# Second-layer matmuls of a fused attention and feed-forward kernel: three passes behind every product, or six behind every second one

## The chip, the cores and the metric

The kernel runs on one core of a Trainium2 chip. The metric is the device time of one execution in microseconds (us). Engines are named as in the profile: PE (TensorE, matmuls), PEld (its weight loads), DVE (VectorE), ACT (ScalarE), SP (SyncE, which issues the DMAs here). A *pass* below is one matmul instruction on PE with 512 moving columns (480 in the last pair of a batch).

## The reference

Four batches of channel attention are followed by a feed-forward layer with GELU:

```python
qn = q / (norm(q, axis=1) + 1e-06); kn = k / (norm(k, axis=1) + 1e-06)   # q, k, v: 4 x 6080 x 256
s = kn.transpose(0, 2, 1) @ qn / tau                                     # 4 x 256 x 256
a = softmax(s, -1)
x = (v @ a).reshape(24320, 256)
h = x @ w_in                                                             # 256 -> 2048
g = 0.5 * h * (1 + erf(h / sqrt(2)))
out = g @ w_out                                                          # 2048 -> 256
```

## The kernel before

The softmax matrix of a batch is multiplied into `w_in` once (`w_group`, line 365), so that the first layer reads the values directly. Every number that goes into a matmul is split into a high and a low part (`vh`/`vl`, `wh`/`wl`, `gh`/`gl`, and `wo[:, 0]`/`wo[:, 1]`), and a product is three passes: low times high, high times high, high times low, added up in one PSUM bank.

**Tiles and loops.** The tokens of a batch are cut into six pairs of two chunks of 512 (480 in the last pair): `j` = 0 and 1. The 2048 hidden channels are cut into eight units of two tiles of 128: `i` = 0 and 1. A step is one batch, pair and unit `(b, p, u)`; there are 192. In a step the first layer computes the four blocks `(i, j)` by `first_products` (line 484), a Strassen-like scheme: seven products of three passes, lines 458 to 460, in banks `one`, `two` and `three` of the PSUM pool `ps_h` (four banks, tile `ph`). Products 1, 2 and 3 are copied to SBUF by ACT (`p1`, `p5`, `u2`, line 491). Products 4, 5 and 6 finish the blocks (1,0), (0,1) and (1,1): DVE adds a kept copy (`h`, line 496). Product 7 finishes (0,0). Product 3 goes into bank `one` again and must wait for the copy of product 1, product 5 for that of product 3, and product 7 for the addition behind product 5. The eight steps of the very first pair use `plain_products` (line 471) instead: eight products, two to a block, in the order (1,0), (0,0), (1,1), (0,1).

**GELU.** `gelu` (line 462) runs on each block: ACT makes the high part `gh` (line 466) and the full `g` (line 467), then DVE the low part `gl` (line 468).

**Second layer.** `second_products` (line 528) is a generator over one step's four blocks. For each chunk `j`, tile `i` and half `c` of the 256 outputs it issues a group of three passes (lines 541 to 543) into one of four banks `po[j, c]` of the pool `ps_o`, which add up over the eight units. A step has eight such groups. At the last unit a finished bank is copied to `osb` (ACT for `c` = 0, line 547, DVE for `c` = 1, line 549) and stored by a DMA that SP issues (line 554).

**What sets the order.** The loop at line 711 runs the products of a step and, behind each, takes one group of the step before from the generator: `next(second, None)`. What is left is drained at line 720. So PE alternates: product, group, product, group. Behind a step come the *extras* (line 653): loads, the next batch's score matmuls (`burst`, lines 191 and 193) with their additions and splits on DVE, `w_group` (lines 376 to 378), norms and the softmax. A scheduler then orders each engine's instructions by the order of writing and by when it expects their inputs, and it inserts the waits. On ACT and DVE it interleaves `h`, `gl` and the rest; on PE it can move single passes.

Of the kernel before, what the change touches and what calls it, by code (L numbers as in the profile page):

```python
# [9 lines left out]
F32 = mybir.dt.float32  # L10
# [6 lines left out]
P = 128  # L17
B, N, C = 4, 6080, 256
DFF = 2048
NT = 512  # L20
NJ = -(-N // P)
NFT = DFF // P
NCT = C // P
# [4 lines left out]
NU = NFT // 2  # L28
# [32 lines left out]
def channel_attention_gelu_ffn(ctx, tc, qk, kqt, vt, tau, w_in, w_out, out):  # L61
# [21 lines left out]
    ps_o = ctx.enter_context(tc.tile_pool(name="ps_o", bufs=4, space=bass.MemoryType.PSUM))  # L83
# [20 lines left out]
    @contextmanager  # L104
    def behind(*names):
        with ExitStack() as stack:
            for name in names:
                stack.enter_context(tc.issue_after(marks[name].ins))
            yield
# [325 lines left out]
    def v_split(b, p, i):  # L435
        n = PAIRS[p][1]
        x = v_blocks(b, p)
        src = {B11: x[0, 0], B21: x[1, 0], B22: x[1, 1]}.get(i)
        if (b, p, i) == (0, 0, B12):
            src = x[0, 1]  # L440
        if src is None:
            src = vts[b, p][i - T1][:, :n]
        hi = pv.tile([P, NT], F32R, name=f"vh{i}")
        lo = pv.tile([P, NT], F32R, name=f"vl{i}")
        nc.scalar.copy(out=hi[:, :n], in_=src)
        nc.vector.tensor_tensor(out=lo[:, :n], in0=src, in1=f32(hi[:, :n]), op=ALU.subtract)
        vops[b, p, i] = hi, lo
# [78 lines left out]
    po = {}  # L526

    def second_products(b, p, u, blocks):

        t0, n = PAIRS[p]  # L530
        wo = wos.pop((b, p, u))
        for j in range(2):
            for i in (1, 0):
                gh, gl = blocks[i, j]
                for c in range(NCT):
                    if u == 0 and i == 1:
                        po[j, c] = ps_o.tile([P, NT], F32, name="po")
                    o = po[j, c][:, :n]
                    cs = slice(c * P, (c + 1) * P)
                    first, last = u == 0 and i == 1, u == NU - 1 and i == 0  # L540
                    nc.tensor.matmul(o, wo[:, 1, i, cs], gh[:, :n], start=first, stop=False)  # L541
                    nc.tensor.matmul(o, wo[:, 0, i, cs], gh[:, :n], start=False, stop=False)  # L542
                    nc.tensor.matmul(o, wo[:, 0, i, cs], gl[:, :n], start=False, stop=last)  # L543
                    if last:
                        if c == 0:
                            osb = pg.tile([P, NCT, NT], F32, name="osb", bufs=2)
                            nc.scalar.copy(out=osb[:, 0, :n], in_=o)
                        else:
                            nc.vector.tensor_copy(out=osb[:, 1, :n], in_=o)
                            t = b * N + t0 + j * n  # L550
                            dst = out[:, t:t + n].rearrange("(t p) n -> p t n", p=P)
                            step = 1 if (b, p) == (B - 1, NP - 1) else NCT
                            for h in range(0, NCT, step):
                                nc.sync.dma_start(out=dst[:, h:h + step], in_=osb[:, h:h + step, :n])
                    yield


    w_in64 = w_in.rearrange("(d p) f -> p d f", p=P)
# [2 lines left out]
    def load_unit():  # L561
        kind, g, d = units.pop(0)
        src = w_in64[:, d, g * NT:(g + 1) * NT] if kind == "in" else w_out64[:, g * 2 * C:(g + 1) * 2 * C]
        loaded.append((kind, g, d, load_w(src)))
# [11 lines left out]
    def narrow_unit():  # L576
        kind, g, d, raw = loaded.popleft()
        if kind == "in":
            if d == 0:
                new_win(0, g)  # L580
            win = wins[0, g]
            narrow(win[:, 0, d], win[:, 1, d], raw)
            if d == NCT - 1:
                keep(keep_in[g], win)
        else:
            new_wo((0, 0, g))
            wo = wos[0, 0, g]
            narrow(wo[:, 0].rearrange("p f c -> p (f c)"), wo[:, 1].rearrange("p f c -> p (f c)"), raw)
            keep(keep_out[g], wo)
# [120 lines left out]
    second = iter(())  # L710
    for b, p, u in steps:
        pair = (b, p + 1) if p + 1 < NP else (b + 1, 0)
        products = plain_products if (b, p) == (0, 0) else first_products
        for i, _ in enumerate(products(b, p, u)):
            next(second, None)
            if u == NU - 1 and pair[0] < B and i < 6:
                v_split(*pair, ORDER[i][1])
        if u == NU - 1 and pair[0] < B:
            v_split(*pair, ORDER[6][1])
        for _ in second:  # L720
            pass
        if (b, p) == (0, 0):
            for _ in range(paces[u] if u < len(paces) else 0):
                with behind(*(["gelu"] if u == 0 else [])):
                    narrow_unit()
                if units:
                    load_unit()
        extras(b, p, u)
        second = second_products(b, p, u, state.pop("blocks"))
# [30 lines left out]
```

## Time and profile before

| what | value |
|---|---|
| time, median of 3 runs | 2186.55 us (2185.65 to 2186.91) |
| time of the profiled execution | 2186.79 us |
| span of its instructions | 2185.0 us |
| PE busy | 2174.5 us (100%), 9664 matmuls |
| PEld busy | 1793.9 us (82%) |
| DVE busy | 1392.8 us (64%) |
| ACT busy | 1437.0 us (66%) |

The time of the profiled execution holds its span and 1.79 us around it. Busy times of PE overlap, since a matmul's end is modelled and the next one starts before it; what a pass costs is the distance from its start to the next start in the timeline.

### The profile page before, as it was taken

The page shows a single profiled execution, that of the slowest core. Times are in us where ns is not written, and L with a number is a line of the kernel's source. Part 1 is how long each engine was busy: PE and PEld are TensorE (multiplying, and loading weights), DVE is VectorE, ACT ScalarE, POOL GpSimd, SP SyncE. Part 2 cuts the span into 40 slices and gives each one's busy share as a digit, 9 for nine tenths or more (in the row PEclk, how much of TensorE's full clock was granted, in tenths as well). Part 3 has the DMA queues.
Part 4 walks back from the last instruction along what each step waited for, and adds up shares of the span by engine and source line. Part 5 has one row for each costly group of instructions (what it writes and reads, how often), then busy time and mean ns, then how long its engine had stood idle before and what let it go on. Part 6 is the DMA issues. An engine that isn't in the chain of part 4 may idle for free.

```text
span 2185.0 us, 26209 instructions
## 1 busy us (share of the span) xinstructions
PE 2174.5 (100%) x9664; PEld 1793.9 (82%) x9664; DVE 1392.8 (64%) x2179; ACT 1437.0 (66%) x2595; POOL 1.3 (0%) x8
## 2 busy tenths in 40 slices
PE   9999999999999999999999999999999999999999
PEld 7788888888888888888888888888888888888888
DVE  6995767656676575675667757657466555555554
ACT  6666666667666666676765666667576566666665
POOL 0000000000000000000000000000000000000000
PEclk9999999999999999999999999999999999999999
DMA  9562534422343353542323335343132122121121
GB/s 380 189 211 106 174 133 157 160 90 87 106 144 105 118 173 116 174 154 67 105 92 134 122 116 174 133 153 128 49 112 97 58 89 71 65 97 66 68 78 47
DMA packets 77056, 267.52 MB, mean 122 GB/s; under 512 B 7680, under 2 KB 9728, under 8 KB 74880
## 3 DMA queue, kind: packets, MB, share of 16 engines
q1 hardware_dynamic: 76928, 265.84, 35.2%
q8 instruction: 76, 1.25, 0.2%
q14 instruction: 52, 0.43, 0.1%
HBM read 232.52 MB, written 33.29 MB: 122 GB/s over the span
## 4 chain that ended last, share of the span: by engine, by line
PE 97%; DVE 2%; DMA 1%; issue 0%; ACT 0%; SPq 0%; DVEq 0%; ACTq 0%
PE po L543 16%; PE po L541 16%; PE po L542 16%; PE ph L460 14%; PE ph L459 14%; PE ph L458 14%; PE ph L191 3%; PE ph L193 1%; DMA raw<-qk 1%; DVE acc L139 1%; PE ph L378 1%; PE ph L376 1%; PE ph L377 1%; PE ph L149 0%; DVE nt L247 0%
## 5 line engine op out<-in xcount | busy, mean ns | idle before, releaser
L468 DVE TENSOR_TENSOR gl<-g,gh 128x512 fp32r<-128x512 f32 (+1 forms) x768 | 521.7, 682 | 145.3 <-ACT g L467 142.7
L543 PE MATMUL po<-gl,wo 128*128 128x512 f32 (+1 forms) x1536 | 605.2, 394 | 0.0
L541 PE MATMUL po<-gh,wo 128*128 128x512 f32 (+1 forms) x1536 | 599.2, 390 | 0.6 <-ACT gh L466 0.6
L542 PE MATMUL po<-gh,wo 128*128 128x512 f32 (+1 forms) x1536 | 595.6, 388 | 0.0
L496 DVE TENSOR_TENSOR h<-ph,p 128x512 f32<-128x512 f32 (+1 forms) x368 | 252.0, 685 | 531.4 <-PE ph L460 452.6
L460 PE MATMUL ph<-vl,wh 128*128 128x512 f32 (+1 forms) x1336 | 522.7, 391 | 0.0
L459 PE MATMUL ph<-vh,wh 128*128 128x512 f32 (+1 forms) x1336 | 521.5, 390 | 0.0
L458 PE MATMUL ph<-vh,wl 128*128 128x512 f32 (+1 forms) x1336 | 519.8, 389 | 0.7 <-DVE wl L363 0.7
L466 ACT ACTIVATE gh<-h 128x512 fp32r<-128x512 f32 (+1 forms) x552 | 345.2, 625 | 236.8 <-DVE h L496 232.8
L491 ACT COPY p<-ph 128x512 f32<-128x512 f32 (+1 forms) x368 | 213.4, 583 | 241.4 <-PE ph L460 240.3
L542 PEld LDWEIGHTS po<-gh,wo 128*128 128x128 f32 x1536 | 288.4, 188 | 64.0
L541 PEld LDWEIGHTS po<-gh,wo 128*128 128x128 f32 x1536 | 288.4, 188 | 62.3 <-ACT gh L466 1.0
L543 PEld LDWEIGHTS po<-gl,wo 128*128 128x128 f32 x1536 | 288.4, 188 | 61.5
L467 ACT ACTIVATE g<-h 128x512 f32<-128x512 f32 (+1 forms) x552 | 337.5, 611 | 0.0
L459 PEld LDWEIGHTS ph<-vh,wh 128*128 128x128 f32 x1336 | 251.1, 188 | 56.9
L458 PEld LDWEIGHTS ph<-vh,wl 128*128 128x128 f32 x1336 | 251.0, 188 | 53.2 <-DVE h L496 1.4
L460 PEld LDWEIGHTS ph<-vl,wh 128*128 128x128 f32 x1336 | 250.9, 188 | 51.0
L491 ACT COPY u<-ph 128x512 f32<-128x512 f32 (+1 forms) x184 | 106.9, 581 | 106.6 <-PE ph L460 106.6
L466 ACT ACTIVATE gh<-ph 128x512 fp32r<-128x512 f32 (+1 forms) x216 | 125.3, 580 | 22.9 <-PE ph L460 18.2
L467 ACT ACTIVATE g<-ph 128x512 f32<-128x512 f32 (+1 forms) x216 | 126.5, 586 | 1.6 <-DVE gl L468 1.5
L496 DVE TENSOR_TENSOR h<-ph,u 128x512 f32<-128x512 f32 (+1 forms) x184 | 125.4, 682 | 2.8
L209 ACT ACTIVATE kqc<-kqc 128x1024 f32<-128x1024 f32 x72 | 76.4, 1061 | 36.1 <-DMA kqc<-kqt 36.0
(135 smaller groups left out, 1354.0 us busy)
## 6 DMA issues: line engine op xcount, KB each, us to landing
wo<-keep_out SPq DMA_DIRECT2D x184, 512.0 KB, 3.3
raw<-qk SPq DMA_DIRECT2D x95, 512.0 KB, 4.3
kqc<-kqt SPq DMA_DIRECT2D x72, 512.0 KB, 4.4
v_raw<-vt SPq DMA_DIRECT2D x20, 1024.0 KB, 5.5
out<-osb SPq DMA_DIRECT2D x40, 512.0 KB, 3.3
win<-keep_in SPq DMA_DIRECT2D x12, 1024.0 KB, 4.8
keep_in<-win SPq DMA_DIRECT2D x4, 1024.0 KB, 4.6
keep_out<-wo SPq DMA_DIRECT2D x8, 512.0 KB, 3.6
```

Of the source, the lines that this page charges most:

```text
L209: nc.scalar.activation(out=x, in_=x, func=AF.Square, accum_out=state["nsum"][:, t, c:c + 1])
L458: nc.tensor.matmul(ps[:, :n], wl, hi[:, :n], start=start, stop=False, skip_group_check=True)
L459: nc.tensor.matmul(ps[:, :n], wh, hi[:, :n], start=False, stop=False, skip_group_check=True)
L460: marks["product"] = nc.tensor.matmul(ps[:, :n], wh, lo[:, :n], start=False, stop=stop, skip_group_check=True)
L466: nc.scalar.activation(out=gh[:, :n], in_=src, func=AF.Gelu)
L467: marks["gelu"] = nc.scalar.activation(out=g[:, :n], in_=src, func=AF.Gelu)
L468: nc.vector.tensor_tensor(out=gl[:, :n], in0=g[:, :n], in1=f32(gh[:, :n]), op=ALU.subtract)
L491: nc.scalar.copy(out=t[:, :n], in_=ps[:, :n])
L496: nc.vector.tensor_tensor(out=h[:, :n], in0=ps[:, :n], in1=t[:, :n], op=ALU.add)
L541: nc.tensor.matmul(o, wo[:, 1, i, cs], gh[:, :n], start=first, stop=False)
L542: nc.tensor.matmul(o, wo[:, 0, i, cs], gh[:, :n], start=False, stop=False)
L543: nc.tensor.matmul(o, wo[:, 0, i, cs], gl[:, :n], start=False, stop=last)
```

## The change

`second_products` now takes chunk `j` = 1 first, and within a chunk it goes through the halves `c` and, inside each, through both tiles `i`. So one call of the generator issues six passes (now lines 542 to 544) into one bank, where it issued three. The tiles of chunk 1 are taken as 0, 1 and those of chunk 0 as 1, 0. The main loop takes a call behind every second product only (`i % 2 == 1`). A step has four calls of six passes in place of eight of three; no instruction is added or dropped.

```diff
--- before.py
+++ after.py
@@ -529,15 +529,16 @@
 
         t0, n = PAIRS[p]
         wo = wos.pop((b, p, u))
-        for j in range(2):
-            for i in (1, 0):
-                gh, gl = blocks[i, j]
-                for c in range(NCT):
-                    if u == 0 and i == 1:
-                        po[j, c] = ps_o.tile([P, NT], F32, name="po")
-                    o = po[j, c][:, :n]
-                    cs = slice(c * P, (c + 1) * P)
-                    first, last = u == 0 and i == 1, u == NU - 1 and i == 0
+
+        for j, tiles in ((1, (0, 1)), (0, (1, 0))):
+            for c in range(NCT):
+                if u == 0:
+                    po[j, c] = ps_o.tile([P, NT], F32, name="po")
+                o = po[j, c][:, :n]
+                cs = slice(c * P, (c + 1) * P)
+                for i in tiles:
+                    gh, gl = blocks[i, j]
+                    first, last = u == 0 and i == tiles[0], u == NU - 1 and i == tiles[1]
                     nc.tensor.matmul(o, wo[:, 1, i, cs], gh[:, :n], start=first, stop=False)
                     nc.tensor.matmul(o, wo[:, 0, i, cs], gh[:, :n], start=False, stop=False)
                     nc.tensor.matmul(o, wo[:, 0, i, cs], gl[:, :n], start=False, stop=last)
@@ -552,7 +553,7 @@
                             step = 1 if (b, p) == (B - 1, NP - 1) else NCT
                             for h in range(0, NCT, step):
                                 nc.sync.dma_start(out=dst[:, h:h + step], in_=osb[:, h:h + step, :n])
-                    yield
+                yield
 
 
     w_in64 = w_in.rearrange("(d p) f -> p d f", p=P)
@@ -712,7 +713,9 @@
         pair = (b, p + 1) if p + 1 < NP else (b + 1, 0)
         products = plain_products if (b, p) == (0, 0) else first_products
         for i, _ in enumerate(products(b, p, u)):
-            next(second, None)
+
+            if i % 2 == 1:
+                next(second, None)
             if u == NU - 1 and pair[0] < B and i < 6:
                 v_split(*pair, ORDER[i][1])
         if u == NU - 1 and pair[0] < B:
```

**A usual step.** On PE, names are output, moving operand and weights: `ph` is a first-layer bank, `po` a second-layer bank; `vh0`, `vh3` are the high parts for products 1 and 2. Before, from a step's first pass:

```order
L458 MATMUL ph_1616<-vh0_1324,wl1_503 128x512
L459 MATMUL ph_1616<-vh0_1324,wh1_502 128x512
L460 MATMUL ph_1616<-vl0_1325,wh1_502 128x512
L541 MATMUL po_1527<-gh_1555,wo_1315 128x512
L542 MATMUL po_1527<-gh_1555,wo_1315 128x512
L543 MATMUL po_1527<-gl_1557,wo_1315 128x512
L458 MATMUL ph_1625<-vh3_1340,wl1_503 128x512
L459 MATMUL ph_1625<-vh3_1340,wh1_502 128x512
L460 MATMUL ph_1625<-vl3_1341,wh1_502 128x512
L541 MATMUL po_1537<-gh_1555,wo_1315 128x512
L542 MATMUL po_1537<-gh_1555,wo_1315 128x512
L543 MATMUL po_1537<-gl_1557,wo_1315 128x512
```

After, the same place:

```order
L458 MATMUL ph_1616<-vh0_1321,wl1_503 128x512
L459 MATMUL ph_1616<-vh0_1321,wh1_502 128x512
L460 MATMUL ph_1616<-vl0_1322,wh1_502 128x512
L458 MATMUL ph_1622<-vh3_1340,wl1_503 128x512
L459 MATMUL ph_1622<-vh3_1340,wh1_502 128x512
L460 MATMUL ph_1622<-vl3_1341,wh1_502 128x512
L542 MATMUL po_1533<-gh_1569,wo_1315 128x512
L543 MATMUL po_1533<-gh_1569,wo_1315 128x512
L544 MATMUL po_1533<-gl_1571,wo_1315 128x512
L542 MATMUL po_1533<-gh_1580,wo_1315 128x512
L543 MATMUL po_1533<-gh_1580,wo_1315 128x512
L544 MATMUL po_1533<-gl_1582,wo_1315 128x512
```

Product 2 moved up to stand directly behind product 1, and the six passes that follow go to one bank and read two blocks.

On DVE, in a usual step of the second batch (`h` with `p1`, `p5`, `u2` are the additions behind products 4, 5 and 6; `gl` the low parts). Before:

```order
L496 TENSOR_TENSOR h_6062<-ph_6058,p1_6036 128x512
L496 TENSOR_TENSOR h_6076<-ph_6032,p5_6045 128x512
L468 TENSOR_TENSOR gl_6066<-g_6065,gh_6064 128x512
L496 TENSOR_TENSOR h_6090<-ph_6041,u2_6053 128x512
L468 TENSOR_TENSOR gl_6080<-g_6079,gh_6078 128x512
L468 TENSOR_TENSOR gl_6094<-g_6093,gh_6092 128x512
L468 TENSOR_TENSOR gl_6106<-g_6105,gh_6104 128x512
```

After:

```order
L496 TENSOR_TENSOR h_6059<-ph_6055,p1_6036 128x512
L468 TENSOR_TENSOR gl_6063<-g_6062,gh_6061 128x512
L496 TENSOR_TENSOR h_6076<-ph_6032,p5_6042 128x512
L496 TENSOR_TENSOR h_6087<-ph_6038,u2_6053 128x512
L468 TENSOR_TENSOR gl_6080<-g_6079,gh_6078 128x512
L468 TENSOR_TENSOR gl_6091<-g_6090,gh_6089 128x512
L468 TENSOR_TENSOR gl_6106<-g_6105,gh_6104 128x512
```

The first `gl`, that of block (1,0), moved ahead of the addition with `p5`, the one for which product 7 waits.

**The start of the first step's second layer.** PE behind the last plain product of step (0, 0, 0); `win`, `eh`, `el` are the operands of `w_group`. Before:

```order
L458 MATMUL ph_586<-vh2_355,wl0_82 128x512
L459 MATMUL ph_586<-vh2_355,wh0_81 128x512
L460 MATMUL ph_586<-vl2_356,wh0_81 128x512
L541 MATMUL po_659<-gh_554,wo_413 128x512
L542 MATMUL po_659<-gh_554,wo_413 128x512
L541 MATMUL po_672<-gh_554,wo_413 128x512
L376 MATMUL ph_629<-win_389,eh_486 128x512
L377 MATMUL ph_629<-win_389,eh_486 128x512
```

After:

```order
L458 MATMUL ph_586<-vh2_355,wl0_82 128x512
L459 MATMUL ph_586<-vh2_355,wh0_81 128x512
L460 MATMUL ph_586<-vl2_356,wh0_81 128x512
L376 MATMUL ph_629<-win_389,eh_486 128x512
L377 MATMUL ph_629<-win_389,eh_486 128x512
L378 MATMUL ph_629<-win_389,el_487 128x512
L376 MATMUL ph_629<-win_389,eh_486 128x512
```

Three second-layer passes that stood ahead of `w_group` moved behind the next two products.

**Where the second batch begins.** PE in step (1, 0, 0), whose second-layer passes are still those of the last pair (480 columns) of the first batch. Before:

```order
L541 MATMUL po_4880<-gh_5538,wo_5258 128x480
L542 MATMUL po_4880<-gh_5538,wo_5258 128x480
L543 MATMUL po_4880<-gl_5540,wo_5258 128x480
L458 MATMUL ph_5617<-vh3_5516,wl0_82 128x512
L459 MATMUL ph_5617<-vh3_5516,wh0_81 128x512
L460 MATMUL ph_5617<-vl3_5517,wh0_81 128x512
L541 MATMUL po_4890<-gh_5538,wo_5258 128x480
L542 MATMUL po_4890<-gh_5538,wo_5258 128x480
L543 MATMUL po_4890<-gl_5540,wo_5258 128x480
L541 MATMUL po_4880<-gh_5590,wo_5258 128x480
L542 MATMUL po_4880<-gh_5590,wo_5258 128x480
```

After:

```order
L542 MATMUL po_4886<-gh_5556,wo_5258 128x480
L543 MATMUL po_4886<-gh_5556,wo_5258 128x480
L544 MATMUL po_4886<-gl_5558,wo_5258 128x480
L542 MATMUL po_4886<-gh_5571,wo_5258 128x480
L543 MATMUL po_4886<-gh_5571,wo_5258 128x480
L458 MATMUL ph_5633<-vh1_5547,wl0_82 128x512
L459 MATMUL ph_5633<-vh1_5547,wh0_81 128x512
L460 MATMUL ph_5633<-vl1_5548,wh0_81 128x512
L544 MATMUL po_4886<-gl_5573,wo_5258 128x480
L458 MATMUL ph_5608<-vh4_5525,wl0_82 128x512
L459 MATMUL ph_5608<-vh4_5525,wh0_81 128x512
L460 MATMUL ph_5608<-vl4_5526,wh0_81 128x512
```

The sixth pass of the first group, which reads the low part of block (1,1), stands three passes later, behind product 4 (`vh1`).

## Rows read from the trace of the kernel before

**Rows 1.** Page: busy time by engine, PE clock by slice, chain that ended last.
```profile
PE 2174.5 (100%) x9664; PEld 1793.9 (82%) x9664; DVE 1392.8 (64%) x2179; ACT 1437.0 (66%) x2595; POOL 1.3 (0%) x8
...
PEclk9999999999999999999999999999999999999999
...
PE 97%; DVE 2%; DMA 1%; issue 0%; ACT 0%; SPq 0%; DVEq 0%; ACTq 0%
```

**Rows 2.** Waits of PE: us in total, times, longest.
```profile
PE ph L149 <- DMA raw<-qk: 4.7, 3, 3.7
...
PE po L541 <- ACT gh L466: 0.6, 1, 0.6
```

**Rows 3.** Groups by line on PE: count, busy us, mean ns, idle before.
```profile
L541 PE MATMUL po<-gh,wo 128*128 128x512 f32 (+1 forms) x1536 | 599.2, 390 | 0.6 <-ACT gh L466 0.6
```

**Rows 4.** Timeline of PE in one step: start us, us, instruction.
```profile
1000.61 0.39 PE L458 MATMUL ph<-vh,wl 128*128 128x512 f32 x1
...
1001.30 0.39 PE L541 MATMUL po<-gh,wo 128*128 128x512 f32 x1
...
1001.76 0.40 PE L543 MATMUL po<-gl,wo 128*128 128x512 f32 x1
1002.00 0.39 PE L458 MATMUL ph<-vh,wl 128*128 128x512 f32 x1
...
1005.21 0.39 PE L460 MATMUL ph<-vl,wh 128*128 128x512 f32 x1
...
1006.59 0.39 PE L460 MATMUL ph<-vl,wh 128*128 128x512 f32 x1
...
1008.89 0.39 PE L458 MATMUL ph<-vh,wl 128*128 128x512 f32 x1
```

**Rows 5.** Timeline of PE: w_group, six passes to each of two banks.
```profile
592.03 0.39 PE L376 MATMUL ph<-win,eh 128*128 128x512 f32 x1
...
593.42 0.39 PE L376 MATMUL ph<-win,eh 128*128 128x512 f32 x1
...
594.80 0.38 PE L458 MATMUL ph<-vh,wl 128*128 128x480 f32 x1
```

**Rows 6.** Timeline of DVE and ACT in the step of rows 4, idle in brackets.
```profile
1005.70 0.69 DVE L496 TENSOR_TENSOR h<-ph,p 128x512 f32<-128x512 f32 x1 [4.08 <-PE ph L460]
...
1006.42 0.63 ACT L466 ACTIVATE gh<-h 128x512 fp32r<-128x512 f32 x1 [1.57 <-DVE h L496]
...
1006.96 0.62 ACT L467 ACTIVATE g<-h 128x512 f32<-128x512 f32 x1
1007.08 0.69 DVE L496 TENSOR_TENSOR h<-ph,p 128x512 f32<-128x512 f32 x1 [0.69 <-ACT gh L466]
...
1007.69 0.68 DVE L468 TENSOR_TENSOR gl<-g,gh 128x512 fp32r<-128x512 f32 x1
```

**Rows 7.** Timeline of DVE and PE around one late product 7.
```profile
883.11 0.69 DVE L496 TENSOR_TENSOR h<-ph,p 128x512 f32<-128x512 f32 x1 [0.65 <-PE ph L460]
...
885.66 0.68 DVE L496 TENSOR_TENSOR h<-ph,p 128x512 f32<-128x512 f32 x1
...
886.06 0.40 PE L543 MATMUL po<-gl,wo 128*128 128x512 f32 x1
...
886.40 0.50 PE L458 MATMUL ph<-vh,wl 128*128 128x512 f32 x1
886.73 0.40 PE L459 MATMUL ph<-vh,wh 128*128 128x512 f32 x1
```

**Rows 8.** Timeline of PE and ACT at the start of the second layer.
```profile
71.31 0.50 PE L541 MATMUL po<-gh,wo 128*128 128x512 f32 x1 [0.56 <-ACT gh L466]
...
72.11 0.40 PE L376 MATMUL ph<-win,eh 128*128 128x512 f32 x1
...
71.16 0.59 ACT L467 ACTIVATE g<-ph 128x512 f32<-128x512 f32 x1
```

**Rows 9.** Timeline of PE and DVE where the second batch begins.
```profile
604.55 0.39 PE L458 MATMUL ph<-vh,wl 128*128 128x512 f32 x1
...
606.58 0.38 PE L541 MATMUL po<-gh,wo 128*128 128x480 f32 x1
606.80 0.38 PE L542 MATMUL po<-gh,wo 128*128 128x480 f32 x1
...
606.85 0.65 DVE L468 TENSOR_TENSOR gl<-g,gh 128x480 fp32r<-128x480 f32 x1
```

## Prediction

> **What bounds the kernel now.** I read the page's busy times first: PE is busy for 2174.5 of 2185.0 us, and the chain that ended last is 97% PE [rows 1]. [...] Next come PE's waits. The first row, 4.7 us, is for the very first loads and is not touched. Of the second layer there is one, 0.6 us, once [rows 2]. So there is almost no idle time to win, and the time is the number of passes times their distance. That distance I read from the timeline of one step: from the first pass of product 1 at 1000.61 to that of product 7 at 1008.89 lie 36 passes, 8.28 us, or 0.230 us each [rows 4]. Last, I look for what stands close behind PE: which inputs arrive just in time, since a new order of passes can only win or lose there, beyond a change of the 0.230 us itself.
>
> **The passes.** The change drops no pass: line 541 stands 1536 times [rows 3], which makes 1536 groups of three before and 768 of six after. What may change is the distance. Before, three passes to one bank alternate with three to another, at 0.230 us. Six passes in a row to one bank are in the trace already, in `w_group`: 592.03 to 593.42 is 1.39 us, and 593.42 to 594.80 is 1.38 us, so 0.230 to 0.232 us each [rows 5]. Alternating takes 1.38 us for six. I take no change. The bounds: 0.005 us more per six passes (the mean of the two `w_group` groups against the alternation) on 768 groups is +3.8 us; and if a change of bank itself cost something, the gain is that of the rival below.
>
> The single steps do differ. From a group's last pass to the next product is 0.24 us (1001.76 to 1002.00), while two steps inside the group take 0.46 us, 0.23 each [rows 4]. But a start can be shown a little early or late without any passage of time, and the sum over a closed round is the same 1.38 us with or without changes of bank [rows 4, 5]. This is why I do not count the 0.01 us as a gain.
>
> **Product 7 in a usual step.** Here the change brings a new order on DVE: the low part `gl` of block (1,0) stands ahead of the addition with `p5`, for which product 7 waits, in some 80 of the 184 steps by the order on DVE. DVE executes in its order, so that addition now waits for ACT too. I place it by the old distances. Product 4 comes three passes, 0.69 us, earlier: its last pass starts at 1005.21 less 0.69, 1004.52; the first addition followed 0.49 later, 1005.01; ACT's `gh` 0.72 behind that, 1005.73; its `g` 0.54 behind, 1006.27, ending 0.62 later, 1006.89; `gl` 0.11 after that, 1007.00; and the next DVE instruction 0.61 behind, 1007.61 [rows 6]. By its own product, whose last pass starts at 1006.59 as before, the addition could start at 1007.08 [rows 4, 6]. So it is half a microsecond later, and ends at 1008.30. Product 7 starts at 1008.89 [rows 4], and the hand-over takes 0.06 us (885.66 + 0.68 to 886.40) [rows 7]. 0.53 us stay spare, so the cost is nothing. The cover is the six passes between products 6 and 7; what it costs without them is the second rival.
>
> Elsewhere in a step, products 2, 4 and 6 come 0.69 us earlier and the others stay, so ACT's copies and GELUs get their inputs earlier or at the same time. Product 3 and product 5 keep their distance to the copies they wait for. The blocks that the second layer now takes first, (0,1) and (1,1), are the later ones, but the first six passes start behind two products instead of one, and (0,0), the last to be ready, is read last.
>
> **Late product 7s.** In four steps product 7 waits today: the start at 886.40 is 0.34 behind the pass before, and the next 0.33, against 0.23 each, so 0.2 us per place [rows 7]; three more look the same. There DVE had stood idle 0.65 us for product 4 [rows 7], which now comes 0.69 us earlier, and the order there already had `gl` first. So these go: -0.8 us. They would stay at worst: 0.
>
> **The start.** Before, PE waits 0.56 us for the first `gh`, runs three passes and begins `w_group` at 72.11 [rows 8]. Now `w_group` comes first, but its bank is that of the first block, which ACT reads until 71.16 + 0.59 = 71.75 [rows 8]; with 0.06 us of hand-over it begins at 71.81. It gains 0.30 us and still owes three passes, 0.69 us: +0.4 us. The wait is not removed, it changes its place. Between 0 and +1 us, as the plain steps behind it are shifted too.
>
> **The batch joints.** There DVE is behind (splits of the next values stand between). The `gl` of block (1,1) ends at 606.85 + 0.65 = 607.50 [rows 9]. In the new order its pass stands behind products 1 and 2 (six passes from 604.55), five passes of the group and product 4: 604.55 + 9 x 0.230 + 5 x 0.22 (606.58 to 606.80) = 607.72 [rows 4, 9]. It is 0.2 us in time. If DVE came half a microsecond later, three joints would cost 1 us. I take 0, bounds 0 and +1.
>
> **The sum.** From the profiled execution's own 2186.79 us (2185.0 and 1.79 around it): -0.8 + 0.4 = 2186.4 us. That execution lies 0.24 us above the median of the three, so against the median the same sum gives 2186.15 us, and I write 2186.2. A measurement of this kernel can tell some 0.2%, 4.4 us, from no change; this is far inside.
>
> **Rivals.** *Changes of bank cost time (faster).* A step goes from 15 changes of bank to 11. If each costs the 0.01 us between 0.24 and 0.23 [rows 4], 4 x 192 x 0.01 = 7.7 us go, at most, and 2178.5 us come out; with half of it, since the display rounds to 0.01, 2182.3 us. Against it stands that six passes to one bank take the same 1.38 us [rows 5]. [...]
>
> *`gl` ahead of the addition makes product 7 late (slower).* The place is DVE in the 80 steps named; it decides from the point where the chain of GELU is 0.53 us longer than worked out. Then each such step pays at least the 0.2 us of a late product 7 [rows 7]: 16 us, 2202 us. For it: DVE is late at product 7 already in four places. Against it: the chain is made of measured distances, and ACT was idle before the first `gh` in the old order (1.57 us) [rows 6]. [...]
>
> *The change does not do what it says.* The scheduler moves single passes, and at the start and the joints some groups of six are split. These are few of 768; the time would be the same, 2186 us.
>
> **How the numbers follow.** My forecast has 0.70, bank changes 0.12, late product 7s 0.10, split groups 0.08. Half of the second case ends over 0.2% below the median (under 2182.2), and a little of the forecast's spread with it: faster 0.09. The third case and the upper end of the distance's bound (2190 and the joints) give slower 0.12. The rest, 0.79, is the same. The forecast's range is 2186.2 less 4 (half of the bank changes) and plus 3.8, 1 and 1, about 6: 2182 to 2192.5. The far half of the bank changes and the late product 7s, 0.16 together, stay outside.
>
> **What would show it.** Right: PE's passes still 0.230 us apart over a step, six passes to one bank in 1.38 us, no new row among PE's waits over 1 us in total, the 0.2 us at the four product 7s gone, `w_group` beginning near 71.8. Wrong: a row "PE ph L458 waits for DVE h" with dozens of times, or a step that takes 0.04 us less than 45 x 0.230 us throughout, which would be the price of the changes of bank after all.

## The result: 4.4 us slower, where no change was forecast

The changed kernel takes 2190.68 us (median of 19 runs, 2188.99 to 2191.92) against 2186.28 us before (19 runs, 2185.55 to 2187.8). The ratio is 1.0019, with a 95% interval of 1.0013 to 1.0025. The profiled execution took 2191.19 us, with a span of 2189.4 us, against 2186.79 and 2185.0. The median lies inside the forecast's range of 2182 to 2192.5 us; what failed is the forecast of no change.

From the page of the changed kernel: busy time by engine, PE clock by slice, and the chain that ended last. The lines answer to [rows 1].

```profile
PE 2177.3 (99%) x9664; PEld 1793.4 (82%) x9664; DVE 1391.3 (64%) x2179; ACT 1421.3 (65%) x2595; POOL 1.3 (0%) x8
...
PEclk9999999999999999999999999999999999999999
...
PE 95%; DVE 2%; DMA 1%; ACT 1%; issue 0%; SPq 0%; DVEq 0%; ACTq 0%
```

PE still bounds the kernel (busy 2177.3 of 2189.4 us), at the same granted clock (a mean of 1.000 before and after), with as many matmuls (9664). All waits of PE after the change, which answer to [rows 2]:

```profile
PE ph L149 <- DMA raw<-qk: 5.6, 4, 3.5
PE ph L376 <- ACT g L467: 1.0, 1, 1.0
PE po L319 <- DVE diag L314: 0.8, 1, 0.8
PE ph L458 <- DVE wl L363: 0.7, 1, 0.7
PE ph L458 <- DVE h L496: 0.4, 1, 0.4
```

The first row belongs to loads ahead of everything that was changed. Behind it, 1.0 us at `w_group` stands in place of the 0.6 for `gh`, and 0.4 for `h` is new: 0.8 us. Most of the rest must lie between passes that wait for nothing. One undisturbed step shows it: the seventh unit of the fifth pair of the second batch, 45 passes of 512 columns, from the first pass of its product 1 to the first pass of the next step's. Before:

```profile
1034.49 0.39 PE L458 MATMUL ph<-vh,wl 128*128 128x512 f32 x1
...
1044.85 0.39 PE L458 MATMUL ph<-vh,wl 128*128 128x512 f32 x1
```

After, the same step:

```profile
1036.26 0.39 PE L458 MATMUL ph<-vh,wl 128*128 128x512 f32 x1
...
1037.64 0.39 PE L542 MATMUL po<-gh,wo 128*128 128x512 f32 x1
...
1039.03 0.39 PE L458 MATMUL ph<-vh,wl 128*128 128x512 f32 x1
...
1046.64 0.39 PE L458 MATMUL ph<-vh,wl 128*128 128x512 f32 x1
```

10.36 us became 10.38 us. This is no chance of one step: worked out from the starts of all passes in the traces, the median step of nearly every unit is 10.360 us before and 10.380 after. Over all 512-column passes without a gap (some 7400) the mean distance is 230.37 ns before and 230.79 after; with 480 columns (1430) it is 216.61 and 217.19. That makes 7400 x 0.42 + 1430 x 0.58 ns = 3.1 + 0.8 = 3.9 of the 4.4 us.

The starts of all passes also say where in a step it goes. Three and three, a product and a group, take 1.380 us before (median). After, six passes of two products take 1.377 us and the six second-layer passes behind them 1.389 (1036.26 to 1037.64 to 1039.03 in the rows). A step has three such rounds of twelve passes, each 0.006 us longer than two rounds of three and three: 0.018 of the 0.020 us. The experiments ask why equal passes, in another order, stand further apart.

### The profile page after: what moved, and what is told of

Read it like the earlier page. It is cut to its first block, busy times and chain, and to the rows that moved or that the text cites. A ratio compares the mean times of both kernels' runs of the same rounds, so it can differ in the third digit from the quotient of the medians.

```text
span 2189.4 us, 26135 instructions
## 1 busy us (share of the span) xinstructions
PE 2177.3 (99%) x9664; PEld 1793.4 (82%) x9664; DVE 1391.3 (64%) x2179; ACT 1421.3 (65%) x2595; POOL 1.3 (0%) x8
## 4 chain that ended last, share of the span: by engine, by line
PE 95%; DVE 2%; DMA 1%; ACT 1%; issue 0%; SPq 0%; DVEq 0%; ACTq 0%
PE po L544 16%; PE po L542 16%; PE po L543 16%; PE ph L459 14%; PE ph L460 14%; PE ph L458 14%; PE ph L191 3%; PE ph L193 1%; DMA raw<-qk 1%; DMA v_raw<-vt 1%; DVE acc L139 1%; PE ph L376 1%; PE ph L378 1%; PE ph L377 1%; ACT gh L466 0%
## 5 line engine op out<-in xcount | busy, mean ns | idle before, releaser
L191 PE MATMUL ph<-hl 128*128 128x512 f32 x272 | 96.0, 392 | 0.0
```

Source lines behind the costliest of these rows:

```text
L191: nc.tensor.matmul(s, hl[:, 0, j, 0, cs], hl[:, :, j, 1], start=(i == 0), stop=False, skip_group_check=True)
```

## The experiments

What they showed first, in one table. *Order* is that of before (three second-layer passes behind each product) or that of the change (six behind two). The next columns say how far the moving operand's start lies ahead of the weights' start in SBUF, by their remainders to 512 bytes, for products and for second-layer passes. The placement is that of the compiled programs. The step is the one shown above.

| kernel | order | products | second layer | step, us | time, us |
|---|---|---|---|---|---|
| before | old | 64 | -64 | 10.36 | 2186.28 |
| changed | new | 64 | -64 | 10.38 | 2190.68 |
| e1_cadence, e3_snake, e4_banks | six behind two | 64 | -64 | 10.38 | 2190.29, 2191.37, 2190.77 |
| e2_order | alternating | 64 | -64 | 10.36 | 2188.98 |
| e5_weights | new | 64 | -64 | 10.38 | 2205.09 |
| e6_moving, e7_shift | new | 64 | 0 | 10.41 | 2195.27, 2195.81 |
| e8_fine | one behind one | 64 | -64 | 10.41 | 2196.91 |
| e9_align_old, units 2 to 7 | old | 0 | 64 | 10.44 | 2193.65 |
| e10_align_new, units 2 to 7 | new | 0 | 64 | 10.25 | 2177.35 |
| e11_even_old | old | 64 | 64 | 10.30 | 2180.59 |
| e12_even_new | new | 64 | 64 | 10.30 | 2180.57 |
| e13_all64_old | old | 64 | -64 | 10.36 | 2186.71 |
| e14_all64_new | new | 64 | -64 | 10.38 | 2190.73 |

In e9_align_old and e10_align_new, units 0 and 1 have 64 and 64, and steps of 10.30 us; the times are those of the whole kernels. A step in the table is the median of such steps, rounded; rows below can differ from it by 0.01 us.

### Neither the bank nor the tiles: the arrangement

**e1_cadence**, from the kernel before:

```diff
-            next(second, None)
+            if i % 2 == 1:
+                next(second, None)
+                next(second, None)
```

> The kernel before with one edit: two calls of the generator behind every second product, so that six second-layer passes stand in a row as in the changed kernel, but in two groups of three to two different banks, and with the old order of tiles and chunks. Theory A (cadence: a second-layer group that stands directly behind another costs about 10 ns more than one behind a product, and a product behind a product about 3 ns less, whichever bank they go to; net about 23 ns per step): about 2190.5 us against 2186.3 before, and twelve passes (six of the first layer, six of the second) in 2.767 us. Theory B (six passes in a row to one bank cost): about 2186.3. Theory C (the new order of tiles and chunks costs, through operands and the waits of other engines): about 2186.3.

Measured: 2190.29 us, ratio 1.0018 (1.0009 to 1.0026). The same step, from timeline rows of PE:

```profile
1035.78 0.39 PE L458 MATMUL ph<-vh,wl 128*128 128x512 f32 x1
...
1046.16 0.39 PE L458 MATMUL ph<-vh,wl 128*128 128x512 f32 x1
```

10.38 us again, though the six passes go to two banks. Theory B, one bank, is out, and so is a price for changes of bank: this kernel has the 15 changes of the old one, and the step of the changed kernel with its 11.

**e2_order**, from the changed kernel: the `yield` stands behind each three passes, and the main loop takes one call behind every product.

```diff
-                yield
+                    yield
...
-            if i % 2 == 1:
-                next(second, None)
+            next(second, None)
```

> The changed kernel with its order of tiles, chunks and halves, but a call of the generator ends behind every three passes and is taken behind every product, so that products and groups of three alternate again. Theory A: about 2186.3 us, twelve passes in 2.760 us. Theory B: about 2186.3, since no six passes to one bank stand together. Theory C: about 2190.7.

Measured: 2188.98 us, ratio 1.001 (1.0001 to 1.0019), between the expectations. The step is the old one (10.37 by the rounded rows, 10.360 as the median of steps):

```profile
1034.98 0.39 PE L458 MATMUL ph<-vh,wl 128*128 128x512 f32 x1
...
1045.35 0.39 PE L458 MATMUL ph<-vh,wl 128*128 128x512 f32 x1
```

The mean distance is 230.37 ns, as before. What is longer, 2.3 us against the kernel before as measured beside it (2186.67), is waits. From the list of PE's waits, where the first row is that of the changed kernel too:

```profile
PE ph L376 <- ACT g L467: 1.0, 1, 1.0
PE ph L458 <- DVE h L496: 0.9, 1, 0.9
...
PE po L542 <- ACT gh L466: 0.7, 1, 0.7
...
PE po L544 <- DVE gl L468: 0.3, 1, 0.3
```

The last three stand within 6 us in the third batch, among the norms. So the new order of tiles costs nothing in the distance of passes; where it alternates, as here, it costs waits.

**e3_snake**, the second tile's three passes reversed:

```diff
+                    passes = [(1, gh), (0, gh), (0, gl)]
+                    if i == tiles[1]:
+                        passes.reverse()
```

> The changed kernel, with the three passes of the second tile of each six in reverse order (high times low, high times high, low times high), so that the passes in the middle of the six are both of the kind high times low. If the extra 10 ns of the second group come from the step between unlike passes in the middle: below 2190, down to 2186.3. Theory A (any second-layer group behind another) and theory B (the bank): about 2190.7 us.

**e4_banks**, the line that creates `ps_h` moved behind that of `ps_o`:

> The changed kernel with the two PSUM pools created in the other order, so that the second layer accumulates in the banks that the first layer had and the other way round. If the place of the banks matters (a second-layer bank with slower access): a time that differs from 2190.7 by over 1 us, and a first-layer product behind a product that gets the extra 10 ns instead. Theories A, B and C: about 2190.7 us.

Measured: 2191.37 us (1.0012 to 1.003 times before) and 2190.77 us (1.0009 to 1.0027), both with a median step of 10.380 us. So neither the middle of the six nor the place of the banks moved the step. So far theory A held: it is the arrangement of products and groups.

### The operands' places

**e5_weights**: `wo[:, 1, i, cs]` and `wo[:, 0, i, cs]` give way to

```diff
+                    w1, w0 = (t[:, (A11, A12, A22, A11)[2 * i + c], u % 2] for t in (wls[u // 2], whs[u // 2]))
```

> The changed kernel, with the weights of every second-layer pass taken from the first layer's weight tiles instead of the loaded second-layer tiles (so the output is not the reference's; number, order, moving operands and banks of the passes stay). After the first four runs theory A stands: six second-layer passes in a row take 1.390 us, six products' passes 1.377, whichever banks they go to. If it is the place of the second layer's weights that makes its passes dear beside each other: six passes in a row near 1.38 us and about 2186.5 us. If it is the moving operand or anything else: 1.390 and about 2190.7.

**e6_moving**: `gh` and `gl` give way to

```diff
+                    gh, gl = (t.rearrange("p a q k -> p (a q k)") for t in (whs[u // 2], wls[u // 2]))
```

> The changed kernel, with the moving operand of every second-layer pass taken from the first layer's weight tiles (512 columns of them) instead of gh and gl (so the output is not the reference's, and PE no longer waits for GELU; weights, order and banks stay). If the place of gh and gl makes the passes dear beside each other: six second-layer passes in a row near 1.38 us and about 2186 us. If it is the weights or anything else: 1.390 and about 2190.

**e7_shift**:

```diff
+    pm.tile([P, 16], F32, name="pad")
     pg = ctx.enter_context(tc.tile_pool(name="pg", bufs=5))
...
-    pwh.tile([P, 16], F32, name="pad")
```

> The changed kernel, with the pool that holds gh, gl and the other GELU tiles moved by 64 bytes in SBUF (a pad of 64 bytes ahead of it in place of the one behind it), nothing else. The start of these tiles was 64 bytes past a multiple of 512, that of the values of the first layer 192 and that of all weights 128. If the place of the moving operand against that of the weights sets the extra time: a different sum for six second-layer passes in a row than 1.390 us, down to 1.38, and down to 2186.5 us. If it is something else: 1.390 and 2190.7.

Measured: 2205.09, 2195.27 and 2195.81 us. The first has the changed kernel's step, 10.380, and its mean distance, 230.79 ns. Of its 14 us, 9.1 stand in the list of PE's waits (17.6 us, against 8.5 after the change), above all in this row:

```profile
PE ph L458 <- ACT p L491: 5.9, 7, 1.9
```

So other weights, in another place but with the same remainder, change nothing in the distance (230.79 ns in both). The moving operand does. The step of e7_shift, whose tiles moved by 64 bytes and whose computation is unchanged:

```profile
1039.13 0.40 PE L458 MATMUL ph<-vh,wl 128*128 128x512 f32 x1
...
1049.53 0.40 PE L458 MATMUL ph<-vh,wl 128*128 128x512 f32 x1
```

10.40 by the rows, 10.407 as the median step, and 231.21 ns per pass. e6_moving reads quite other tiles, with the same remainder of 128, and has 231.22 ns and a median step of 10.407 too. So the start of the operand counts, and as far as these two placements show it counts by its remainder. The 64 bytes are worth more than the change itself (0.027 us per step, where the change made 0.020).

**e8_fine** asked whether theory A holds in itself: one second-layer pass behind every pass of a product, so that hardly any stand together.

```diff
         nc.tensor.matmul(ps[:, :n], wl, hi[:, :n], start=start, stop=False, skip_group_check=True)
+        next(state["second"], None)
```

(the same behind the other two passes, and a `yield` behind each second-layer pass)

> The kernel before, with one second-layer pass behind every pass of a product instead of three behind three; the last three of a step still stand together. If what costs is only that second-layer passes stand behind one another: a mean distance of passes below the 0.2304 us of before, some 0.2300, and about 2184 us or less. If a change between the two kinds costs anything: over 0.2304 us and over 2187. Waits may come in, since a product now ends two passes later; they would show as rows among PE's waits.

Measured: 2196.91 us, ratio 1.0045 (1.0031 to 1.0059). The step is 10.41:

```profile
1041.18 0.39 PE L458 MATMUL ph<-vh,wl 128*128 128x512 f32 x1
...
1051.59 0.39 PE L458 MATMUL ph<-vh,wl 128*128 128x512 f32 x1
```

The passes are 231.25 ns apart; of the rest of the time, 1.8 us are one wait for `h` in PE's list. That is against theory A, by which separating the second-layer passes should have helped. Three and three is better at these placements (10.36 us); "behind one another is dear" is no rule.

### Theory D: starts and order together

**e9_align_old** and **e10_align_new**: the kernel before, and the changed one, with

```diff
+    pm.tile([P, 32], F32, name="pad")
     pg = ctx.enter_context(tc.tile_pool(name="pg", bufs=5))
...
-    pwh.tile([P, 16], F32, name="pad")
```

> The kernel before, with the pool of gh, gl and the other GELU tiles moved by 128 bytes (a pad ahead of it, the pad behind it dropped), so that gh and gl start 192 bytes past a multiple of 512, as the first layer's values do, instead of 64; the weights of units 2 to 7 move by 64 bytes too, those of units 0 and 1 and of the second layer don't. Theory D (the distance of passes is set by where the moving operand of a pass and of its neighbours start, 64, 128 or 192 bytes past a multiple of 512; the changed order costs because it makes other pairs neighbours): with all starts alike, the order of passes no longer matters, so this and the next kernel have the same mean distance, to 0.0001 us, somewhere near the 0.2300 us that sixteen products' passes in a row take, and some 2184 us each. Theory A (second-layer passes behind one another cost as such): this one keeps its lead of 0.0004 us per pass over the next.

> The changed kernel with the same shift by 128 bytes. Theory D: the same mean distance as the kernel above, to 0.0001 us. Theory A: 0.0004 us per pass more, some 4 us in all. If the units 0 and 1, whose weights did not move, differ from the others in it, the start of the weights matters too.

Measured: 2193.65 us (ratio 1.0033, 1.0021 to 1.0045) and 2177.35 us (0.996, 0.9948 to 0.9973). Both theories are wrong on the total, since the drop of the pad moved the weights of units 2 to 7 as well. But the units tell the two apart. In e9_align_old, first a step of unit 0 (its last row is the first score matmul that follows the 45 passes), then the step of unit 6:

```profile
969.05 0.39 PE L458 MATMUL ph<-vh,wl 128*128 128x512 f32 x1
...
979.35 0.40 PE L191 MATMUL ph<-hl 128*128 128x512 f32 x1
...
1036.74 0.40 PE L458 MATMUL ph<-vh,wl 128*128 128x512 f32 x1
...
1047.18 0.40 PE L458 MATMUL ph<-vh,wl 128*128 128x512 f32 x1
```

In e10_align_new the same two steps:

```profile
963.48 0.39 PE L458 MATMUL ph<-vh,wl 128*128 128x512 f32 x1
...
973.78 0.39 PE L191 MATMUL ph<-hl 128*128 128x512 f32 x1
...
1030.80 0.39 PE L458 MATMUL ph<-vh,wl 128*128 128x512 f32 x1
...
1041.06 0.39 PE L458 MATMUL ph<-vh,wl 128*128 128x512 f32 x1
```

Unit 0, where values and GELU tiles start alike and all weights do: 10.30 us in both orders. Unit 6, where the first layer's weights start elsewhere: 10.44 in the old order and 10.26 in the new (10.254 as the median step). The sign of the change turns with the placement of the tiles.

**e11_even_old** and **e12_even_new** make all units like unit 0, with the pools in another order:

```diff
-    pg = ctx.enter_context(tc.tile_pool(name="pg", bufs=5))
     pwh = ctx.enter_context(tc.tile_pool(name="pwh", bufs=1))
...
+    pwh.tile([P, 16], F32, name="pad2")
+    pg = ctx.enter_context(tc.tile_pool(name="pg", bufs=5))
```

> The kernel before, with the pool of the first layer's weights created ahead of the pool of the GELU tiles and a pad of 64 bytes between them: gh and gl start 192 bytes past a multiple of 512 like the first layer's values, and all weights at 128. Theory D, as the last two runs left it (the starts of moving operands and weights set the distance; where both layers have the same starts, the order of the passes does not matter): every step of 45 passes with 512 columns takes 10.300 us, as it did in units 0 and 1 of the last two, against 10.360 before; some 152 such steps, so about 9 us less, less up to 2 us for the passes with 480 columns: 2177 to 2179 us. Theory A (the alternation is better as such): steps shorter than those of the next kernel by 0.02 us or more.

> The changed kernel with the same placement. Theory D: steps of 10.300 us too, and the same time as the kernel above within 1 us but for waits (about 0.5 us more at the start). Theory A: steps longer by 0.02 us or more, some 4 us in all.

Measured: 2180.59 and 2180.57 us, both 0.9975 of before (0.9964 to 0.9985). The step of unit 6 in the one, then the other:

```profile
1030.52 0.39 PE L458 MATMUL ph<-vh,wl 128*128 128x512 f32 x1
...
1040.82 0.39 PE L458 MATMUL ph<-vh,wl 128*128 128x512 f32 x1
```

```profile
1030.58 0.39 PE L458 MATMUL ph<-vh,wl 128*128 128x512 f32 x1
...
1040.88 0.39 PE L458 MATMUL ph<-vh,wl 128*128 128x512 f32 x1
```

10.30 us twice, and the 4.4 us between the two orders are gone. This is what decides for theory D. The times are 1.6 us above the upper end of what was expected. The 480-column passes explain a part: 218.3 against 216.6 ns, 1430 times, is +2.4 us where up to 2 had been allowed. The rest was not traced.

**e13_all64_old** and **e14_all64_new** move everything together:

```diff
+    const.tile([P, 16], F32, name="pad0")
     whs = [const.tile([P, 7, 2, P], F32R, name="wh0")]
```

> The kernel before, with a pad of 64 bytes ahead of all tiles, so that every moving operand and every weight tile starts 64 bytes further and keeps its distance from all others. If the starts count only against each other: steps of 10.360 us and 2186.3 us, as before. If their place in memory counts as such: another step.

> The changed kernel with the same pad of 64 bytes ahead of all tiles. If the starts count only against each other: steps of 10.380 us and 2190.7 us. If their place in memory counts as such: another step, and the difference of 0.020 us to the kernel above need not hold.

Measured: 2186.71 us (ratio 1.0, 0.9991 to 1.0009) and 2190.73 us (1.0018, 1.0009 to 1.0028). The old order's step, then the new one's (lines are one further):

```profile
1032.68 0.39 PE L459 MATMUL ph<-vh,wl 128*128 128x512 f32 x1
...
1043.04 0.39 PE L459 MATMUL ph<-vh,wl 128*128 128x512 f32 x1
```

```profile
1036.06 0.39 PE L459 MATMUL ph<-vh,wl 128*128 128x512 f32 x1
...
1046.44 0.39 PE L459 MATMUL ph<-vh,wl 128*128 128x512 f32 x1
```

10.36 and 10.38, as without the pad. With this one common shift, the starts count against each other and not by their place.

**What stays open** is the mechanism: no run says what, inside a pass of equal length, costs the few nanoseconds. Nor do the runs separate which starts count against each other: a pass's moving operand against its own weights, as the table is laid out, or against the operands of the passes beside it. Both kinds of tile matter, since moving the GELU tiles alone changed the step (10.38 to 10.41 us in e7_shift), and so did moving the first layer's weights alone (10.44 and 10.25 us in units 2 to 7, against 10.30 in units 0 and 1, in e9_align_old and e10_align_new). The remainder to 512 bytes describes all fourteen runs; a smaller modulus isn't excluded, nor were other distances than -64, 0 and 64 tried. The fastest version is e10_align_new, the change with a pad of 128 bytes: 0.4% faster than the kernel before.

## Why the prediction was wrong, point by point

**The passes: the step that failed.** "I take no change" was the mis-sized term: it was 3.9 us. Its upper bound, +3.8, was the right size, by luck, and with it the upper end of the range: it was read from `w_group` [rows 5], whose six passes were taken for a stand-in because they go to one bank. The bank turned out not to matter (10.38 us in e1_cadence and e4_banks, as in the changed kernel). What matters, the starts of the operands against each other (10.25 to 10.44 us), was looked at nowhere: in `w_group` the moving operand starts 64 bytes ahead of the weights, by remainders of 128 and 64, and in the second layer 64 behind. A second error was one of resolution: 36 passes in 8.28 us [rows 4] were read as 0.230 us "with or without changes of bank", but the effect is 0.4 ns per pass. Over six passes that is lost in the display's 0.01 us; only whole steps, or all of them, could have bounded it.

A nearer stand-in than `w_group` stood in the trace of before and was not read. The last two groups of every step are drained one behind the other, so six second-layer passes stand in a row there, in the step of [rows 4] too:

```profile
1009.58 0.39 PE L541 MATMUL po<-gh,wo 128*128 128x512 f32 x1
...
1010.97 0.40 PE L191 MATMUL ph<-hl 128*128 128x512 f32 x1
```

That is 1.39 us; over the trace the median is 1.389, against 1.380 for three and three. The change makes three more such rows of six in a step.

**Product 7 in a usual step: right, in the mechanism too.** No row of dozens of waits for `h` came up; there is one, 0.4 us. The count was low: in the trace of after, `gl` stands ahead of the addition with `p5` in 103 of the 184 steps (4 before), not in some 80. One of them, DVE and then PE:

```profile
1008.65 0.69 DVE L468 TENSOR_TENSOR gl<-g,gh 128x512 fp32r<-128x512 f32 x1 [1.22 <-ACT g L467]
1009.26 0.68 DVE L496 TENSOR_TENSOR h<-ph,p 128x512 f32<-128x512 f32 x1
...
1010.64 0.39 PE L458 MATMUL ph<-vh,wl 128*128 128x512 f32 x1
```

The addition ends at 1009.94, 0.70 us ahead of product 7. Less the hand-over of 0.06 that is 0.64 us to spare, where 0.53 had been worked out. That DVE keeps to its order shows in the next rows.

**Late product 7s: wrong in sum.** They were to go (-0.8). Three of the four did, but the one near 886 grew, and two came up elsewhere. Timeline of DVE and then PE around it, which answers to [rows 7]:

```profile
885.40 0.69 DVE L427 TENSOR_TENSOR vs<-v_raw 128x512 f32<-128x512 f32 x1 [1.21 <-DMA v_raw<-vt]
886.01 0.68 DVE L550 COPY osb<-po 128x512 f32<-128x512 f32 x1
...
887.21 0.68 DVE L496 TENSOR_TENSOR h<-ph,p 128x512 f32<-128x512 f32 x1
...
884.39 0.39 PE L544 MATMUL po<-gl,wo 128*128 128x512 f32 x1
...
887.15 0.39 PE L544 MATMUL po<-gl,wo 128*128 128x512 f32 x1
887.95 0.51 PE L458 MATMUL ph<-vh,wl 128*128 128x512 f32 x1 [0.40 <-DVE h L496]
```

DVE stands 1.21 us for a load of the next values. It keeps to its order meanwhile: the copy to `osb`, next behind, has its bank finished at 884.39 + 0.39 = 884.78 and starts at 886.01. So the addition, further behind, ends at 887.21 + 0.68 = 887.89. The prediction had removed the wait for product 4 there and not asked what stands next in DVE's order. By the gaps over 0.23 us the late product 7s are 1.3 us after and 0.8 before: +0.5 in place of -0.8. They differ from kernel to kernel; in e1_cadence PE's list has 0.2 us for `h`, against 0.4 in the changed kernel.

**The start: right.** Timeline of PE and ACT, which answers to [rows 8]:

```profile
71.30 0.50 PE L376 MATMUL ph<-win,eh 128*128 128x512 f32 x1 [1.04 <-ACT g L467]
...
70.65 0.59 ACT L467 ACTIVATE g<-ph 128x512 f32<-128x512 f32 x1
```

`w_group` begins 0.06 us behind the end of ACT's reading (70.65 + 0.59 = 71.24), as worked out; this execution was half a microsecond earlier as a whole. The wait grew from 0.56 to 1.04 us: +0.5 against the +0.4 taken.

**The batch joints: right (0).** The scheduler split one group there and put product 4 ahead of its last pass.

**The sum.** 3.9 for the passes, +0.5 for the start and +0.5 for the product 7s make 4.9, against 4.4 between the profiled executions. The other -0.5 lies ahead of all that was changed. The first plain product, before and then after:

```profile
64.94 0.50 PE L458 MATMUL ph<-vh,wl 128*128 128x512 f32 x1 [0.67 <-DVE wl L363]
```

```profile
64.43 0.50 PE L458 MATMUL ph<-vh,wl 128*128 128x512 f32 x1 [0.67 <-DVE wl L363]
```

The start of this product lies between 63.2 and 65.2 us over the sixteen traces, so the -0.5 is put down to the executions and not to the change.

**The rivals.** Changes of bank cost nothing that the step shows (10.38 us with 15 of them in e1_cadence, and with 11 in the changed kernel). `gl` ahead of the addition made nothing late in usual steps. Few groups are split: 750 times exactly six second-layer passes stand in a row, of 768 groups. The true cause was not among the rivals.

## What to carry to other kernels

When PE has no idle time, an order of passes can still cost or give back time through the distance of passes (here 0.42 ns each, 3.9 us in all with the 480-column passes), and this distance must be taken from whole steps, or from the mean over thousands, not from a few rows that are shown to 0.01 us. In these runs a row could stand in for a pass only where its operands started alike, moving operand against weights (otherwise 10.41 us in place of 10.38, e7_shift), and where the same kind of pass stood beside it (otherwise 10.41 in place of 10.36, e8_fine). An order that wins or loses some tenths of a per cent is worth measuring again with the tiles moved by 64 and 128 bytes: here the pad decided the sign (the change made +0.02 us a step without it, and -0.19 in units 2 to 7 with it).

## What the hardware showed that was not expected

The same 45 passes, without any wait and at the same granted clock (0.999 to 1.000 in every run), took from 10.25 to 10.44 us, by order and placement alone: 1.8%. With both layers placed alike they took 10.30 in either order. There is no single value for a pass of 512 columns: the means of whole kernels are 228.5 to 231.3 ns. The runs don't show whether a pass waits for anything inside it, but they do show that it matters where its operands start (10.38 us became 10.41 in e7_shift, where nothing but the start of the GELU tiles changed, by 64 bytes).

At 480 columns the best placement is another: 216.6 ns per pass in the kernel before, but 218.2 in e10_align_new, which is the fastest at 512 columns (228.5 ns).
